# Queries and keys of the first 512 positions read eight tokens to a partition, in half-height loads, with a new order of the first part

## The chip, the cores and the metric

One core of a Trainium2 chip runs the kernel. The metric is the time of one execution in device microseconds (us), the median of several runs. A profile is one further execution, recorded by the hardware; its engines are PE (TensorE: matmuls, with PEld its weight loads), DVE (VectorE), ACT (ScalarE), POOL (GpSimd) and SP (SyncE, here a queue of DMA issues).

## What is computed

Attention over 4 batches of 8 heads, 768 positions and 64 numbers to a head, in which a query sees the first four positions (sinks) and the last 128 up to itself; the heads are put beside one another (512 numbers to a position), and two layers with a squared ReLU between them follow.

```python
def _attn_ref(q, k, v, n_sink, window):        # q, k, v: 4, 8, 768, 64; n_sink 4, window 128
    scores = scale * np.matmul(q, k.transpose(0, 1, 3, 2))
    keep = is_sink | in_window
    scores = np.where(keep, scores, -1000000000.0)
    a = np.exp(scores - np.max(scores, axis=-1, keepdims=True))
    a = a / (np.sum(a, axis=-1, keepdims=True) + 1e-09)
    return np.matmul(a, v)

def _moe_ref(x, w_in, w_out):                  # x: 3072, 512; w_in: 512, 2048; w_out: 2048, 512
    r = np.maximum(x @ w_in, 0.0)
    return (r * r) @ w_out
```

All inputs and the output are float32; the kernel multiplies in bfloat16.

## The kernel before

The four batches run one behind another, with the attention of a batch beside the two layers of the batch before it. Batch 0 has nothing to run beside, so its first part is the kernel's start.

**How batch 0 starts.** Its queries and keys come in two groups: positions 0 to 511 (four tiles of 128) are loaded as float32 by SP into the tiles qr, all others as bfloat16 by POOL into qn. A head pair m (two heads, 0 to 3) is handled together. For the first 512 positions the steps are: eight loads on SP (line 351), keys and queries by turns for each pair, 256 KB each; a cast and regrouping of each into qs (`regroup`, line 478, recorded as the copies at lines 192 and 194); four 128x128 transposes on PE for each (`transpose`, line 507); and a copy out of PSUM into qkT (`unload`, line 522), which also puts the tokens back in order. Then come, for each block of 256 queries (s = 0 for the first, s = 1 for the second): the scores on PE (line 613; in block 0 a bias is first added by a matmul with the identity, line 606), the exponential on ACT (line 634), in block 1 a mask on POOL or DVE (lines 218 and 646), the product with the values on PE (line 682), the normalisation on DVE (lines 698 and 699), two transposes called bridges (line 731) with copies into xT. The sink keys (line 549) and the sinks' scores and exponential (lines 572 and 580) serve block 1 onward.

**The layers.** Layer 1 (line 763) of batch 0 runs in groups of 16 matmuls: four blocks of 128 hidden numbers by 256 positions. There are eight groups for blocks 0 and 1, and the quarter of w_in (line 308) that a group needs is loaded by POOL. Layer 2 of batch 0 (line 984) starts behind them, and then the layers of batch 1 and the rest.

**What sets the order.** Every step is numbered as it is declared, and `ORDER` lists the numbers in the order in which the instructions are written, over all engines. Each engine runs its own instructions in that order, and semaphores come in where a step needs another's result. A letter behind a number chooses the engine (d DVE, a ACT, g POOL, p PE), and "+" the pool of PSUM banks ("att" or "den", two each). A bank is free when its readers are done, so the order also decides who waits for whom over banks. `DUMMIES` puts idle matmuls ahead of some steps (29 in step 945, ten ahead of 63, eight ahead of 58, four ahead of 64, three each ahead of 83, 91 and 97); they keep PE busy and compute nothing.

The steps that are spoken of, by number (m is the pair):

| step | what | step | what |
|---|---|---|---|
| 8 to 15 | the eight loads into qr | 83, 84, 91, 92 | scores of block 0, m = 0, 1, 2, 3 |
| 55, 61, 67, 73 | cast of keys, m = 0 to 3 | 85, 86, 93, 94 | their exponentials |
| 56, 62, 68, 74 | cast of queries | 87, 89, 95, 97 | their values; 88, 90, 96, 98 norms |
| 57, 63, 69, 75 | transposes of keys | 103, 104, 113, 114 | scores of block 1, m = 0, 1, 2, 3 |
| 58, 64, 70, 76 | transposes of queries | 105, 107, 115, 117 | their exponentials |
| 59, 65, 71, 77 | unloads of keys | 106, 108, 116, 118 | their masks |
| 60, 66, 72, 78 | unloads of queries | 109, 111, 119, 121 | their values |
| 80, 81, 82 | sink keys, scores, exponential | 99, 101; 100, 102 | bridges of block 0; their copies |
| 4, 5, 2, 127 | triangles, bias masks (POOL), second constants (DVE), mask tables (POOL) | 156, 162, 168 | first, second, third group of layer 1 |
| 19 to 25, 26 | v loads and w_in's first three quarters, its last | 177 | first group that needs w_in's last quarter |
| 37 to 44, 49 to 52 | key and query loads of batch 1 | 45 to 48 | v loads of batch 1 |
| 144, 136, 145 | scores of block 2 | 146, 148; 149 | exponentials and a mask of block 2 |
| 278 | start of layer 2 | 248, 251 | last transposes of batch 1's queries and keys |

One load, before: 128 partitions, in each two heads with four tokens of 64 numbers, so rows of 1 KB in memory. Two pairs lie beside one another in a tile of 128 x 4 x 256.

Of the kernel before, what the change touches and what calls it, by code (L numbers as in the profile page):

```python
# [21 lines left out]
944 0 1 2 7 8 9 10 11 12 13 14 15 16 17 18 945+0 3 5 19 20 21 6 79 22 23 24 25 55d 56d 57+0 58 59d 60a 83+0 85 103+1  # L22
105 26 27 28 62d 61d 63+1 64 67d 68d 65a 69+0 70 71d 72d 66a 84+1 73a 74a 75+1 76 78d 91+0 86 77a 93 80 113+1 87+0
92+1 89 94 95+0 97 115 88 90 96 98 114+1 99+0 101 117 100d 104+0 81+1 102d 107 82 4 29 106g 30 31 32 33 34 35 36 37 38
39 40 41 42 43 44 45 46 127 47 48 49 50 116d 118d 108d 156+0 109+1 119+1 121 111 162+0 110 120 122 112 123+1 125 124d
126d 157a 163a 158a 164a 168+1 165+0 51 52 53 54 177+0 169a 170d 208g 166a 167a 178d 171+1 179a 172a 128+1 131+0 174+0
173a 132a 129d 319 323 321 175d 324 176d 322 130a 320 159+1 133a 160a 161a 278+0 279 136+1 144+0 145+0 280 281 148 138
146 289+1 149d 139d 274 147d 275 282 290 283 291 292 284 276 277 134+1 137+0 135 286a 140 141d 285 287d 293 150+0 151
294 142+1 196+0 192+1 295 143 193 200+1 198a 202a 195d 197 199d 201 203d 297d 194d 296 298a 152+1 154 204+0 205
# [87 lines left out]
def kernel(  # L117
# [59 lines left out]
    def bank(slot, name, shape, dtype):  # L177

        return rooms[slot.pool][slot.room].tile(shape, dtype, name=name, tag=f"{slot.pool}{slot.room}")
# [153 lines left out]
    def load_qk(b, m0, ti, g, pairs=2, behind=None, yields=()):  # L333
# [10 lines left out]
        def run(e):  # L344
            if half == 0:
                qr_t[share] = bank(qr_slot[share], "qr", [128, shares * 2 * pairs, n * D], FP32)
            t = qr_t[share][:, 2 * pairs * half:2 * pairs * half + 2 * pairs, :]
            qr_t[b, "all", m0, ti, g] = t
            for m in range(m0, m0 + pairs):
                qr_t[b, m, ti, g] = t[:, 2 * (m - m0):2 * (m - m0) + 2, :]  # L350
            return [nc.sync.dma_start(  # L351
                out=t,
                in_=(q, k)[ti][b, 2 * m0:2 * m0 + 2 * pairs, t0:t0 + 128 * n, :].rearrange(
                    "h (p t) d -> p h (t d)", t=n))]
# [72 lines left out]
    def attention(b, key):  # L427
# [16 lines left out]
        def stage(g, f0, f1, side):  # L444
# [25 lines left out]
            for m in range(0, NP, w) if b not in NATURAL else ():  # L470
# [4 lines left out]
                for ti in () if casted else (1, 0):  # L475
                    sl = qs_slot[b, m, ti, g] = Slot("qs", 1)

                    def regroup(e, m=m, ti=ti):
                        t = qs_t[b, m, ti, g] = bank(qs_slot[b, m, ti, g], "qs", [128, w, n, 2, D], BF16)
                        if w == 2:  # L480
                            copy(e, t, qr_t[b, "all", m, ti, g].rearrange("p (m h) (t d) -> p m t h d", m=2, d=D))
                        else:
                            copy(e, t[:, 0], qr_t[b, m, ti, g].rearrange("p h (t d) -> p t h d", d=D))
                    who = {"pool": 0.17 + w * n * 0.125}
                    who["dve"] = 0.06 + w * n * (0.094 if b else 0.115)
                    if w == 1:
                        who["act"] = 0.2 + w * n * 0.107
                    regs.append(op(at(f), who, regroup,
                                   after=[ops["qk", b, m, ti, g]] + prev_tr + begun, takes=[sl],
# [31 lines left out]
                for j in (1, 0):  # L521
                    def unload(e, m=m, j=j, casted=casted):
# [9 lines left out]
                        else:  # L532
                            ins = copy(e,
                                       qkT_sb[:, m, j, t0 // 128:last // 128, :].rearrange(
                                           "c a b -> c (a b)").rearrange("c (p t) -> c p t", t=n),
                                       bank_t[b, m, g][:, j, 0:128 * n].rearrange("c (t p) -> c p t", t=n))
# [3 lines left out]
                    for x in ((m + j,) if w == 2 else (m,)):  # L540
                        ops.setdefault(("copies", b, x, g), []).append(c)
# [742 lines left out]
    for m in range(NP):  # L1284
        for ti in (1, 0):
            load_qk(0, m, ti, 0, 1)
# [114 lines left out]
```

## Time and profile before

| | us |
|---|---|
| median of 3 runs | 210.08 (209.55 to 211.03) |
| the profiled execution | 210.16 |
| its span (first to last instruction) | 208.3 |

| engine | busy us | share |
|---|---|---|
| PE | 200.5 | 96% |
| DVE | 173.1 | 83% |
| ACT | 135.9 | 65% |
| POOL | 96.4 | 46% |

The granted TensorE clock is 1.00 over the span. 1.9 us of the profiled execution lie around its span. Times in a view count from the span's start. The chain of waits is followed back from the last instruction, each step to what released it; an engine's name means that the engine was working, DMA that a transfer was awaited. PE's busy time is modelled at the ends of matmuls, so gaps of a few hundredths are not seen.

POOL's share of the start, which sets when its loads go out (columns: start, length, engine, line, work, count):

```profile
1.70 0.77 POOL L218 TENSOR_SCALAR_AFFINE_SELECT sg<-sg 128x256 bf16<-128x256 bf16 x2
2.53 0.61 POOL L254 COPY sg<-sg 128x512 bf16<-128x512 bf16 x1
3.45 2.16 POOL L381 DMA_DIRECT2D v<-in_v_dram  x2
5.61 0.76 POOL L308 DMA_DIRECT2D w_in_sb<-in_moe_w_in_dram  x1
10.69 2.25 POOL L308 DMA_DIRECT2D w_in_sb<-in_moe_w_in_dram  x3
```

### The profile page before, as it was taken

What the parts mean: (1) busy time and instruction counts of PE and PEld (TensorE: products, weight loads), DVE (VectorE), ACT (ScalarE), POOL (GpSimd) and SP (SyncE); (2) the same over time, 40 slices, a digit from 0 to 9 for tenths busy, and PEclk for the clock granted to TensorE, in tenths of its full rate; (3) what the DMA queues carried; (4) which work ended last, traced back from release to release, by engine and by line L of the source; (5) the groups of instructions that cost most, each with busy time, mean ns of one, the idle gap of its engine ahead of it and who ended that gap; (6) DMA issues with size and microseconds to landing.
All of it is one profiled execution on the core that took longest, in us unless ns stands there. A gap on an engine that the chain in (4) does not pass through costs nothing.

```text
span 208.3 us, 5924 instructions
## 1 busy us (share of the span) xinstructions
PE 200.5 (96%) x2476; PEld 174.3 (84%) x2476; DVE 173.1 (83%) x318; ACT 135.9 (65%) x189; POOL 96.4 (46%) x138
## 2 busy tenths in 40 slices
PE   7989999999998999999999998999999999999993
PEld 7658997457986889989878987999888999998893
DVE  6759268867599998999999987999989598999933
ACT  2695888433749589999987047988856248693110
POOL 7999274599599976689356209000043000000000
PEclk9999999999999999999999999999999999999999
DMA  6999999999999999999999945300204203200115
GB/s 190 260 184 207 173 196 215 166 146 142 261 68 148 131 172 137 181 162 121 154 116 220 109 96 134 148 3 0 50 14 145 50 5 113 88 3 0 50 54 201
DMA packets 93994, 26.10 MB, mean 125 GB/s; under 512 B 86800, under 2 KB 91408, under 8 KB 93968
## 3 DMA queue, kind: packets, MB, share of 16 engines
q0 software_dynamic: 69248, 12.59, 80.2%
q1 hardware_dynamic: 24536, 13.01, 27.9%
q8 instruction: 19, 0.31, 0.6%
q10 hardware_dynamic: 184, 0.14, 0.2%
q14 instruction: 7, 0.06, 0.1%
HBM read 27.30 MB, written 6.29 MB: 161 GB/s over the span
## 4 chain that ended last, share of the span: by engine, by line
PE 82%; DVE 5%; DMA 4%; SPq 3%; ACT 2%; issue 2%; DVEq 0%; ACTq 0%
PE py L1233 26%; PE pm L894 23%; PE pm L763 10%; PE py L984 7%; PE po L682 6%; PE ps L613 4%; DMA qr<-in_q_dram 3%; PE pt L507 2%; PE py L1094 2%; SPq L351 2%; DVE t L936 1%; PE px L731 1%; DMA xT<-xn_sb 1%; SPq L461 1%; ACT expm L634 1%
## 5 line engine op out<-in xcount | busy, mean ns | idle before, releaser
L634 ACT ACTIVATE expm<-ps 128x1024 bf16<-128x1024 f32 (+1 forms) x48 | 43.7, 953 | 7.7 <-PE ps L613 7.5
L218 POOL TENSOR_SCALAR_AFFINE_SELECT expm<-expm 128x512 bf16<-128x512 bf16 x34 | 22.7, 705 | 44.2 <-ACT expm L634 40.4
L894 PEld LDWEIGHTS <-w_in_sb 128*128 128x128 bf16 x384 | 32.2, 114 | 2.0 <-issue 1.9
L1233 PEld LDWEIGHTS <-gT_sb 128*128 128x128 bf16 x288 | 27.2, 98 | 4.7 <-issue 1.4
L917 ACT ACTIVATE gT_sb<-r 128x1024 bf16<-128x1024 bf16 x28 | 28.8, 1054 | 2.5 <-DVE r L963 2.3
L894 PE MATMUL pm<-xs,wi 128*128 128x256 bf16 (+1 forms) x288 | 29.2, 246 | 0.1
L192 ACT ACTIVATE osb<-py 128x256 f32<-128x256 f32 (+1 forms) x30 | 11.9, 399 | 25.0 <-PE py L1233 19.8
L936 DVE TENSOR_TENSOR t<-t,pm 128x512 f32<-128x512 f32 x36 | 23.8, 683 | 3.7 <-PE pm L894 2.9
L894 PEld LDWEIGHTS <-wi 128*128 128x128 bf16 x288 | 24.6, 114 | 1.0 <-DVE xs L852 0.4
L1233 PEld LDWEIGHTS <-sg 128*128 128x128 bf16 x216 | 20.3, 98 | 2.7 <-issue 0.5
L963 DVE CUSTOM_DVE_ANT_1 r<-pm,t 128x1024 bf16<-128x1024 f32 x18 | 21.8, 1218 | 0.5 <-PE pm L894 0.5
L763 PE MATMUL pm<-xT,w_in_sb 128*128 128x256 bf16 x192 | 22.0, 273 | 0.0
L763 PEld LDWEIGHTS <-w_in_sb 128*128 128x128 bf16 x192 | 20.6, 114 | 0.3 <-issue 0.2
L894 PE MATMUL pm<-xs,w_in_sb 128*128 128x256 bf16 (+1 forms) x192 | 19.9, 246 | 1.0 <-DVE t L936 1.0
L951 ACT ACTIVATE r<-pm 128x1024 bf16<-128x1024 f32 x16 | 16.3, 1022 | 4.9 <-DVE osb L194 2.3
L1233 PE MATMUL py<-w_out_sb,gT_sb 128*128 128x256 bf16 x144 | 18.7, 273 | 0.6 <-ACT expm L634 0.6
L1233 PE MATMUL py<-wt,sg 128*128 128x256 bf16 x144 | 18.7, 273 | 0.0
L1233 PE MATMUL py<-wt,gT_sb 128*128 128x256 bf16 x144 | 18.5, 273 | 0.0
L682 PEld LDWEIGHTS <-expm 128*128 128x128 bf16 x352 | 16.6, 97 | 1.9 <-issue 0.6
L682 PE MATMUL po<-v,expm 128*128 128x65 bf16 x352 | 17.8, 193 | 0.3 <-ACT expm L634 0.3
L699 DVE TENSOR_TENSOR xn_sb<-po,rc 128x512 bf16<-128x512 f32 (+1 forms) x28 | 17.2, 615 | 1.0
L984 PE MATMUL py<-w_out_sb,gT_sb 128*128 128x512 bf16 x64 | 14.8, 379 | 0.0
(104 smaller groups left out, 376.9 us busy)
## 6 DMA issues: line engine op xcount, KB each, us to landing
out_dram<-osb SPq DMA_DIRECT2D x11, 512.0 KB, 3.7
v<-in_v_dram POOLq DMA_DIRECT2D x24, 128.0 KB, 6.2
qn<-in_k_dram POOLq DMA_DIRECT2D x20, 128.0 KB, 6.1
qn<-in_q_dram POOLq DMA_DIRECT2D x20, 128.0 KB, 6.5
w_in_sb<-in_moe_w_in_dram POOLq DMA_DIRECT2D x4, 512.0 KB, 9.4
w_out_sb<-in_moe_w_out_dram POOLq DMA_DIRECT2D x4, 512.0 KB, 10.8
qr<-in_k_dram SPq DMA_DIRECT2D x4, 256.0 KB, 5.1
qr<-in_q_dram SPq DMA_DIRECT2D x4, 256.0 KB, 4.8
```

What stands on the lines that cost most here:

```text
L218: nc.gpsimd.affine_select(out=e_tile, in_=e_tile, compare_op=ALU.is_ge, fill=fill, base=i - 1, pattern=[[0, n], [1 if i else -1, 128]], ch ...
L634: nc.scalar.activation(out=x[:, :, o:512], in_=bank_t["s", b, s, m][:, :, o:512], func=AF.Exp, scale=scale)
L682: touch(("po", b, s, m0), e, nc.tensor.matmul(pv[:, i, h2, :], lhsT=lhsT, rhs=rhs, start=(n_ == 0), stop=(n_ == len(mms) - 1)), j)
L699: touch(("po", b, s, m0), e, nc.vector.tensor_tensor(out=xn_sb[:, 2 * s:2 * s + 2, 128 * (m0 + j0):128 * (m0 + j0 + nj)].rearrange("p i (j ...
L763: nc.tensor.matmul(pm[:, i, :], lhsT=w_in_sb[:, fb // 4, kb, fb % 4:512:4], rhs=xT[:, c0 // 256:(c0 + cw) // 256, kb, :], start=(kb == 0), ...
L894: touch(tag, e, nc.tensor.matmul(y[:, bk, i, :], lhsT=weights(name, f0 + i, a), rhs=rhs[:, a, :], start=fresh and i == 0 and a == 0, stop= ...
L917: nc.scalar.activation(out=d, in_=x, func=AF.Square)
L936: touch(tag, e, nc.vector.tensor_tensor(out=T["t"], in0=T["t"], in1=T["y"][:, bk], op=ALU.subtract), bk)
L951: touch(tag, e, nc.scalar.activation(out=r, in_=T["y"], func=AF.Relu), 0, 1)
L963: touch(tag, e, nc.vector._custom_dve(TENSOR_ADD_SAT, out=r.rearrange("p b n c -> p b (n c)"), in0=T["y"].rearrange("p b n c -> p b (n c)" ...
L984: touch((b, u), e, nc.tensor.matmul(pm[:, i, :], lhsT=gT_sb[:, fb, 128 * t:128 * t + 128], rhs=w_out_sb[:, fb, :], start=(fb == 0), stop=( ...
L1233: touch((b, u), e, nc.tensor.matmul(region(name), lhsT=x[:, i, :], rhs=w_[:, i, :], start=first and i == 0, stop=i == HB - 1, skip_group_c ...
```

## The change

Three things are changed for positions 0 to 511 of batch 0.

The loads: one load now writes 64 partitions, in each two heads with eight tokens of 64 numbers, so rows of 2 KB. A tile of 128 x 2 x 512 holds the keys, or the queries, of two pairs: the even pair in partitions 0 to 63, the odd one in 64 to 127. There are still eight loads of 256 KB, now in the order keys of pairs 0 and 1, queries of 0 and 1, keys of 2 and 3, queries of 2 and 3.

The steps on them: a cast, its four transposes and its unload now take half of the tokens of each partition (the first four of eight, or the last four) of both pairs in the tile, where they took all tokens of one pair. A cast waits for two loads, and the scores of a pair wait for four unloads where they waited for two. An unload writes four tokens of every eight, for two pairs.

The order: `ORDER` is new up to its 191st step and the same from there. `DUMMIES` is not changed, so the idle matmuls go with their steps. The instructions on PE are the same in number.

```diff
@@ -19,14 +19,14 @@
 ORDER = """
-944 0 1 2 7 8 9 10 11 12 13 14 15 16 17 18 945+0 3 5 19 20 21 6 79 22 23 24 25 55d 56d 57+0 58 59d 60a 83+0 85 103+1
-105 26 27 28 62d 61d 63+1 64 67d 68d 65a 69+0 70 71d 72d 66a 84+1 73a 74a 75+1 76 78d 91+0 86 77a 93 80 113+1 87+0
-92+1 89 94 95+0 97 115 88 90 96 98 114+1 99+0 101 117 100d 104+0 81+1 102d 107 82 4 29 106g 30 31 32 33 34 35 36 37 38
-39 40 41 42 43 44 45 46 127 47 48 49 50 116d 118d 108d 156+0 109+1 119+1 121 111 162+0 110 120 122 112 123+1 125 124d
-126d 157a 163a 158a 164a 168+1 165+0 51 52 53 54 177+0 169a 170d 208g 166a 167a 178d 171+1 179a 172a 128+1 131+0 174+0
-173a 132a 129d 319 323 321 175d 324 176d 322 130a 320 159+1 133a 160a 161a 278+0 279 136+1 144+0 145+0 280 281 148 138
-146 289+1 149d 139d 274 147d 275 282 290 283 291 292 284 276 277 134+1 137+0 135 286a 140 141d 285 287d 293 150+0 151
-294 142+1 196+0 192+1 295 143 193 200+1 198a 202a 195d 197 199d 201 203d 297d 194d 296 298a 152+1 154 204+0 205
+8 9 10 11 12 13 14 944 15 0 4 945+0 7 16 1 3 6 19 20 21 5 62d 56d 61a 55a 63+0 57+1 64 58 65a 59a 66a 60a 73d 75+0 77a
+67d 68d 74d 69+0 104+1 103+1 76 70 107 105 71d 84+1 22 79 23 24 25 106g 108g 78d 72d 2 86 83+0 80 85 91+1 93 92+0 87+1
+89 81+1 113+0 94 88 90 95+0 97 82 115 96 98 114+1 117 26 118g 27 28 29 30 31 32 116d 99+1 109+0 101 111 119+0 102d
+100a 156+1 120 121 112 110 122 162+1 123+0 125 319 322 323 126a 124a 168+0 157a 169a 163d 324 320 321 159+0 158a 170d
+160a 165+1 177+0 166a 167d 174+1 128+1 171+1 178d 129d 161d 130a 164a 175d 172d 176d 33 34 208g 35 131+1 278+0 279
+133a 132a 179a 280 281 36 37 38 39 40 41 42 144+1 136+0 145+0 146 148 138 173a 149g 43 44 45 46 47 48 127 282 283 147d
+274 275 276 277 289+1 290 284 17 18 139d 49 50 51 52 53 54 291 292 134+1 137+0 135 286a 140 141d 285 287d 293 150+0
+151 294 142+1 196+0 192+1 295 143 193 200+1 198a 202a 195d 197 199d 201 203d 297d 194d 296 298a 152+1 154 204+0 205
 212+0+1 153a 155d 189+0 215 206a 213 190a 214 207d 186+0 216 191d 248+0 187d 249d 251+1 209 253a 188d 252a 180+1 181d
 250d 182d 183+0 326 184a 185d 300 301 230+0+1 233 299 288 219+0+1 231 220 304+0 210+0 306a 211 222 305 237+0+0 240
 232d 325 302 221 303 223 241d 238 239d 311 307 217+1 254+0 224+0 308a 255 309 218 242+0 225 243 452g 422 423 424 425
@@ -343,15 +343,12 @@
 
         def run(e):
             if half == 0:
-                qr_t[share] = bank(qr_slot[share], "qr", [128, shares * 2 * pairs, n * D], FP32)
-            t = qr_t[share][:, 2 * pairs * half:2 * pairs * half + 2 * pairs, :]
-            qr_t[b, "all", m0, ti, g] = t
-            for m in range(m0, m0 + pairs):
-                qr_t[b, m, ti, g] = t[:, 2 * (m - m0):2 * (m - m0) + 2, :]
+                qr_t[share] = bank(qr_slot[share], "qr", [128, 2, 2 * n * D], FP32)
+            qr_t[b, m0, ti, g] = qr_t[share]
             return [nc.sync.dma_start(
-                out=t,
-                in_=(q, k)[ti][b, 2 * m0:2 * m0 + 2 * pairs, t0:t0 + 128 * n, :].rearrange(
-                    "h (p t) d -> p h (t d)", t=n))]
+                out=qr_t[share][64 * half:64 * half + 64],
+                in_=(q, k)[ti][b, 2 * m0:2 * m0 + 2, t0:t0 + 128 * n, :].rearrange(
+                    "h (p t) d -> p h (t d)", t=2 * n))]
         o = dma_op("sp", ("qk", b, m0, ti, g), run, 16 * pairs * ROW[256 * n] + (0.7 if (b, m0, ti, g) == (0, 0, 0, 0) else 0.0), behind,
                    () if half else [qr_slot[share]], yields)
         for m in range(m0, m0 + pairs):
@@ -477,16 +474,14 @@
 
                     def regroup(e, m=m, ti=ti):
                         t = qs_t[b, m, ti, g] = bank(qs_slot[b, m, ti, g], "qs", [128, w, n, 2, D], BF16)
-                        if w == 2:
-                            copy(e, t, qr_t[b, "all", m, ti, g].rearrange("p (m h) (t d) -> p m t h d", m=2, d=D))
-                        else:
-                            copy(e, t[:, 0], qr_t[b, m, ti, g].rearrange("p h (t d) -> p t h d", d=D))
+                        x = qr_t[b, m, ti, g].rearrange("p h (t d) -> p t h d", d=D)
+                        copy(e, t[:, 0], x[:, n * (m % 2):n * (m % 2) + n])
                     who = {"pool": 0.17 + w * n * 0.125}
                     who["dve"] = 0.06 + w * n * (0.094 if b else 0.115)
                     if w == 1:
                         who["act"] = 0.2 + w * n * 0.107
                     regs.append(op(at(f), who, regroup,
-                                   after=[ops["qk", b, m, ti, g]] + prev_tr + begun, takes=[sl],
+                                   after=[ops["qk", b, m // 2 * 2 + i, ti, g] for i in range(2)] + prev_tr + begun, takes=[sl],
                                    reads=[qr_slot[b, m, ti, g]]))
                     ops["regroup", b, m, ti, g] = regs[-1]
 
@@ -530,14 +525,16 @@
                                            "c i a b -> c i (a b)").rearrange("c i (p t) -> c i p t", t=n),
                                        bank_t[b, m, g][:, j, 0:256 * n].rearrange("c (i t p) -> c i p t", i=2, t=n))
                         else:
+                            mm, half = m // 2, m % 2
                             ins = copy(e,
-                                       qkT_sb[:, m, j, t0 // 128:last // 128, :].rearrange(
-                                           "c a b -> c (a b)").rearrange("c (p t) -> c p t", t=n),
-                                       bank_t[b, m, g][:, j, 0:128 * n].rearrange("c (t p) -> c p t", t=n))
+                                       qkT_sb[:, 2 * mm:2 * mm + 2, j, t0 // 128:last // 128, :].rearrange(
+                                           "c m a b -> c m (a b)").rearrange("c m (p t) -> c m p t", t=2 * n)
+                                       [:, :, :, n * half:n * half + n],
+                                       bank_t[b, m, g][:, j, 0:128 * n].rearrange("c (t m p) -> c m p t", t=n, m=2))
                         touch(("pt", b, m, g), e, ins, j, alone=True)
                     c = op(at(f + 0.04), {"dve": 0.42 if casted else 0.11 + w * n * 0.144, "act": 0.17 + w * n * 0.107}, unload,
                            after=[trs[j]] + prev_scores + prev_sinks, reads=[bs])
-                    for x in ((m + j,) if w == 2 else (m,)):
+                    for x in ((m + j,) if w == 2 else (m // 2 * 2, m // 2 * 2 + 1)):
                         ops.setdefault(("copies", b, x, g), []).append(c)
                     copies.append(c)
 
@@ -1281,9 +1278,10 @@
     FAST = {1: ((0, 1), (2,)), 2: ((0,), (1, 2)), 3: ((0,), (1, 2))}
     CLASSIC2 = ((0, 0), (0, 1))
     load_sinks("act", 0)
-    for m in range(NP):
+    for mm in range(0, NP, 2):
         for ti in (1, 0):
-            load_qk(0, m, ti, 0, 1)
+            for m in (mm, mm + 1):
+                load_qk(0, m, ti, 0, 1)
     for b in range(1, B):
         load_sinks("sp", b)
     load_v(0, 0, None, [("qk", 0, 3, 0, 0)])
```

## The prediction

> **What bounds the kernel now.** I read the page first: the engines' busy time and the chain that ended last.
>
> ```profile
> PE 200.5 (96%) x2476; PEld 174.3 (84%) x2476; DVE 173.1 (83%) x318; ACT 135.9 (65%) x189; POOL 96.4 (46%) x138
> PE 82%; DVE 5%; DMA 4%; SPq 3%; ACT 2%; issue 2%; DVEq 0%; ACTq 0%
> ```
>
> TensorE is the bound nearly everywhere; the 4% of DMA is where the change works. The chain in order of time shows that place.
>
> ```profile
> 3.97 0.47 SPq L351
> 4.44 0.04 issue
> 4.48 6.15 DMA qr<-in_q_dram
> ...
> 10.72 0.64 ACT qs L192
> ...
> 11.40 0.40 PE pt L507 x4
> ...
> 13.76 0.82 ACT expm L634
> ...
> 16.62 1.87 PE pm L763 x16
> 18.50 1.45 PE po L682 x48
> 19.95 1.75 PE pm L763 x16
> 21.70 0.45 PE px L731 x8
> 22.15 6.99 PE pm L763 x64
> ```
>
> Columns: start, length, work. The eighth and last load of queries (issued at 4.48) lands at 10.63. Call this moment L. Until 16.6 the chain passes between ACT, PE and DVE; from 16.62 on it is PE alone. The third layer-1 group starts at 22.15, L + 11.52. The busy time by stretches says that PE is then full:
>
> ```profile
> 4.00:6.00 2.00, 2.00 (x22) 2.00 (x20) 1.05 (x3) 0.00 (x0) 2.00 (x3) 1.00 1.01 307
> 6.00:8.00 2.00, 2.00 (x28) 1.36 (x25) 0.98 (x2) 1.23 (x2) 1.73 (x6) 1.00 1.11 306
> 16.00:36.00 20.00, 20.00 (x239) 18.36 (x238) 13.58 (x26) 15.31 (x18) 11.92 (x16) 1.00 1.49 198
> 36.00:56.00 20.00, 20.00 (x192) 12.64 (x191) 12.87 (x21) 9.83 (x15) 15.95 (x23) 1.00 2.20 175
> 55.00:56.00 1.00, 1.00 (x11) 1.00 (x10) 0.81 (x2) 1.00 (x3) 0.22 (x1) 1.00 1.04 422
> ```
>
> The second figure is PE's busy time, the last the GB/s moved. PE is busy for all of 16 to 56. The order is the same in both programs from about 46 us on, and both do the same matmuls before that. So what the change is worth is how much earlier or later the third layer-1 group starts; behind it, both have five more groups (1.75 each) and 0.9 of transposes before layer 2 (33.52 before). The rest follows from two terms: L, and the work from L to that group.
>
> **The work behind L.** Before, the last load feeds one head pair; the seven other loads have already been cast, turned and partly exponentiated. In the new program each cast takes half of the tokens of two pairs, so both query casts of pairs 2 and 3 need both of the last two query loads. Behind L stand in series:
> - two casts on DVE (steps 68, 74; four took 2.20): 1.10;
> - eight transposes, of which PE issues 0.45, then the two bias matmuls (0.33) and the scores of step 84 (0.17, and 0.23 to its end), with 0.07 to each next engine: about 1.25. ACT can start step 86 at L + 2.35;
> - then ACT without a gap: exponentials 86, 85, 93, 94 (start to start 0.70 on 11.25 to 11.94), sink keys 80 (0.43), sink exponential 82 (0.38), exponentials 115 and 117 (four in 3.61 up to 17.37, one of them 0.70: 0.97 each) and the copy 100 (0.59): 2.80 + 0.43 + 0.38 + 1.94 + 0.59 = 6.14.
>
> I checked that nothing arrives later than ACT asks for it: the three unloads on DVE (0.60 each) end at L + 2.95, the sink keys ask at L + 3.05; the scores 91 and 92 are ready 0.25 before their exponentials. Step 100 gates the first layer-1 group, at L + 8.5. Then 1.75 + 0.36 (one values step) + 1.75 + 0.45 (two bridges): the third group starts at L + 12.8. That is 1.3 later than now for the same L: the new order has nine ACT steps and three of the four values steps of the second block between L and layer 1, where the old one has six and none.
>
> **L itself.** The eight loads are 2.10 MB, moved from about 2.2 at 306 GB/s until 9.05; landing is 1.6 behind. The count of SP issues (eight of 0.47) stays; two kinds of change pull apart:
> - Rows twice as long (2 KB for 1 KB). The nearest rows are the w_in loads, read in 2 KB rows: the second, third and fourth land at 18.7, 21.4 and 24.5, 1.05 MB in 2.9 us, 362 GB/s. At that rate 5.8 for 6.85. The v loads go out 0.65 earlier (they no longer stand behind the bias masks on POOL), which takes back some 0.3: L = 9.9.
> - Each load writes 64 partitions instead of 128. No row shows a large load of that shape. If the write side of a half is half as wide, the bound is half of the best rate in the trace, 422 / 2 = 211 GB/s: 9.95 us, L = 2.2 + 9.95 + 1.6 = 13.7.
>
> The low end is all 2.10 MB at 422: L = 8.8; no load can land before its issue plus the shortest seen, 4.48 + 2.75 (first load, issue 0.81, cast 3.56) = 7.2. Between 9.9 and 13.7 no row decides. I take 13.7: the loads go down one queue one behind another, lower half, upper half, so all engines write the same half at the same time. [...]
>
> **Parts that cost nothing, and their cover.**
> - The warm-up matmuls now read the triangles and so start 0.5 later, behind two POOL selects (0.55): the first transposes wait for K casts after 4.5 anyway. The idle matmuls keep their step numbers (ten ahead of step 63) and run while loads fly.
> - Unloads write four of every eight tokens. The nearest rows are 0.60 (strided, today) and 0.41 (contiguous). Up to 0.2 more each: three on DVE behind L, of which 0.1 is covered, so 0 to +0.5; I take 0.
> - Second constants (0.9 on DVE) move behind the unloads; the next DVE step waits for values until L + 4.6, they end at L + 3.8.
> - w_in's last quarter is issued behind two POOL masks (1.70 for two selects each), near 16.2 instead of 12.2. It stands behind 6.3 MB anyway, lands by about 24.5, and is asked for three groups after the third, at L + 18.
> - The key and query loads of batch 1 now stand on POOL behind the mask of step 149, which waits for exponential 148. Counted from the start of layer 2: 148 ends at +5.8, the mask takes 1.7, two loads 1.8, four v loads 3.6, the mask tables 2.3, three loads 2.6, and the last lands 5.1 later (as 48.9 to 54.0 now): +22.9. The transposes that need it stand at 56.44 - 33.52 = +22.9. Covered with nothing to spare: 0 taken, bounds 0 and +1.
>
> **Sum.** L later by 3.1, work behind it 1.3: +4.4 on the profiled execution's 210.16, 214.6; that run is 0.08 above the median of 210.08, so 214.5.
>
> **Rivals.**
> - *Full rate into half the partitions.* L = 9.5 to 10.6, so 1.3 less 1.1 to 1.3 less 0: +0.2 to +1.3, and 211 at the middle. For it: all 16 engines carry each load, and today's 306 GB/s is below the 422 that they reach. Against it: the shape is not in the trace. In this case the longer rows gain nearly a microsecond and the order gives it back.
> - *Faster.* Loads become so quick that the order's tail is paid for. Place: the landing of the eighth load; it decides from L below 9.3. At 8.8 the gain is 1.83 - 1.3 = 0.5, 209.5; at the floor of 7.2 it is 2.1, 207.9. For it: 2 KB rows, and today v loads share the engines from 4.5 on. Against it: over 1% needs the floor itself, and from the fourth load on none landed less than 4.6 after its issue.
> - *POOL is late.* Loads at full rate, but POOL's chain to batch 1's last query load (22.9 against 22.9) or the strided unloads bite: +0.6 for the first case and 1.0 to 1.5 more, 212.3. POOL's 4.9 us of waits on w_out's DMAs speak for a tight queue; that DMA falls idle after 57 speaks against a long delay.
>
> **Chances.** I call 1% (2.1 us) what a measurement of this kernel tells from no change. Half rate 0.56, with 212.6 to 216; full rate 0.30; POOL late 0.08; faster 0.06, half of it by over 1%. Faster by over 1%: 0.03. Within 1%: 0.30 + 0.03 + 0.02 of the half-rate case = 0.35. Slower: 0.54 + 0.08 = 0.62. The likeliest case alone spans 213.5 to 215.8; the full-rate case needs its lower part, so the range is 210.2 to 215.9, leaving out the faster rival, the best of the full rate and L beyond 15.
>
> **What would show it.** Right: the wait on the last qr load ends near 13.7, ACT's first exponential of the first block follows 2.3 to 2.4 later, the third layer-1 group starts 12.8 behind the landing, and GB/s in 4 to 8 is near 211 instead of 306. If GB/s is 306 or more there and the landing is near 10, the half-rate step is wrong and the time is near 211. If the third group starts less than 11.5 behind the landing, the order's term has the wrong sign. If PE waits at the pt transposes of qn near 57, POOL is late. If the time falls below 208, a step above hid a wait that the new order removes.

## The result and the profile after

| | before | after |
|---|---|---|
| median, us | 210.48 (209.55 to 211.28, 6 runs) | 217.75 (216.84 to 218.48, 6 runs) |
| ratio to before | | 1.0346, 95% interval 1.0305 to 1.0388 |
| the profiled execution, us | 210.16 | 217.33 |
| last qr load landed (L) | 10.63 | 15.24 |
| third layer-1 group starts | 22.15 | 29.60 |
| from there to the end of the execution | 188.0 | 187.7 |

The change makes the kernel 7.3 us slower. The last row says where: nothing is lost behind the third group, and the whole loss lies in the first 30 us.

The page of the profile after, its busy times and its shares of the chain:

```profile
PE 202.5 (94%) x2476; PEld 174.8 (81%) x2476; DVE 172.8 (80%) x315; ACT 134.1 (62%) x189; POOL 101.1 (47%) x144
PE 84%; DMA 6%; SPq 4%; DVE 3%; issue 1%; ACT 1%; DVEq 0%
```

PE is busy for 2.0 us longer with the same 2476 matmuls. DMA's share of the chain has grown from 4% to 6%, by about the 4.6 us that L moved. The chain in order of time (start, length, work) shows both:

```profile
5.55 9.69 DMA qr<-in_q_dram
...
16.25 1.03 PE pt L502 x8
17.28 0.64 PE ps L603 x2
...
25.29 1.75 PE pm L760 x16
...
27.40 1.75 PE pm L760 x16
...
29.60 8.73 PE pm L760 x80
```

L is 5.55 + 9.69 = 15.24, and the third group starts 14.36 behind it. From 16.25 to beyond that group the chain is on PE without a break; two bias matmuls (line 603) take 0.64. The busy time by stretches (the stretch, its length, PE, PEld, DVE, ACT, POOL, then the granted clock of PE, the DMA engines' busy share, GB/s) says why they take so long:

```profile
4.00:6.00 2.00, 1.98 (x19) 1.71 (x17) 0.00 (x0) 0.33 (x1) 2.00 (x4) 1.00 1.05 234
6.00:8.00 2.00, 0.35 (x4) 0.23 (x4) 0.00 (x0) 1.99 (x3) 1.88 (x5) 1.00 1.51 197
...
10.00:12.00 2.00, 0.00 (x0) 0.00 (x0) 0.00 (x0) 0.38 (x1) 2.00 (x4) 1.00 1.35 194
12.00:14.00 2.00, 1.00 (x12) 0.75 (x14) 0.86 (x2) 0.44 (x1) 0.69 (x1) 0.78 1.17 217
...
16.00:18.00 2.00, 1.75 (x12) 1.11 (x14) 1.90 (x4) 0.47 (x1) 1.39 (x3) 0.50 2.17 163
18.00:20.00 2.00, 2.00 (x16) 0.79 (x13) 1.05 (x4) 1.22 (x4) 1.71 (x3) 0.51 1.32 205
```

In 4 to 6 the engines were as busy as before (1.05 against 1.01) and moved 234 GB/s in place of 307. PE has nothing to do from 9.8 to 13.0, waiting for casts of loads that have not landed; from 13.1 to 20 its clock is granted at half, and the work behind L begins in the midst of that. Over 4 to 10, first before, then after:

```profile
4.00:10.00 6.00, 5.98 (x69) 4.71 (x67) 3.96 (x9) 3.23 (x6) 5.67 (x11) 1.00 1.27 280
```

```profile
4.00:10.00 6.00, 3.95 (x47) 3.28 (x45) 1.07 (x2) 4.25 (x7) 5.68 (x12) 1.00 1.39 197
```

### The profile page after: what moved, and what is told of

Read it like the earlier page. It is cut to its first block, busy times and chain, and to the rows that moved or that the text cites. A ratio compares the mean times of both kernels' runs of the same rounds, so it can differ in the third digit from the quotient of the medians.

```text
span 215.3 us, 5936 instructions
## 1 busy us (share of the span) xinstructions
PE 202.5 (94%) x2476; PEld 174.8 (81%) x2476; DVE 172.8 (80%) x315; ACT 134.1 (62%) x189; POOL 101.1 (47%) x144
## 3 DMA queue, kind: packets, MB, share of 16 engines
q1 hardware_dynamic: 23512, 13.01, 28.3%
## 4 chain that ended last, share of the span: by engine, by line
PE 84%; DMA 6%; SPq 4%; DVE 3%; issue 1%; ACT 1%; DVEq 0%
PE py L1230 25%; PE pm L891 23%; PE pm L760 10%; PE po L679 7%; PE py L981 7%; DMA qr<-in_q_dram 4%; PE ps L610 4%; PE pt L502 2%; SPq L348 2%; PE py L1091 2%; PE px L728 1%; DMA xT<-xn_sb 1%; PE ps L603 1%; SPq L458 1%; SPq L710 1%
## 5 line engine op out<-in xcount | busy, mean ns | idle before, releaser
L218 POOL TENSOR_SCALAR_AFFINE_SELECT expm<-expm 128x512 bf16<-128x512 bf16 x40 | 27.9, 731 | 55.1 <-ACT expm L631 52.2
L610 PE MATMUL ps<-qkT 64*128 64x128 bf16 (+1 forms) x256 | 15.1, 246 | 0.4 <-ACT r L772 0.4
```

The lines of the kernel that those rows point to most:

```text
L218: nc.gpsimd.affine_select(out=e_tile, in_=e_tile, compare_op=ALU.is_ge, fill=fill, base=i - 1, pattern=[[0, n], [1 if i else -1, 128]], ch ...
L610: nc.tensor.matmul(ps[:, h2, o:o + w], lhsT=qkT_sb[r, m, 1, c, :], rhs=qkT_sb[r, m, 0, qb:qb + w // 128, :], start=(i == 0 and not biased) ...
```

## The experiments

Three explanations were to be told apart: the loads are slow because they write 64 partitions, or because of their long rows, or because of what else is in flight in the new order; and what stands behind L is long because of the order, or because of PE's clock. Each landing, and each start of the third group, is read from one execution, the profiled one. The changed kernel and e6, which load alike, differ by 0.24 in the landing (15.24 and 15.48). The start of the third group scatters more: e2, e9 and e12 have the median time of before, but their profiled executions, which were among the slowest of theirs, start it at 23.59 to 23.77, where that of before has 22.15. Smaller differences than these say little by themselves; the ratios rest on several executions each.

**Half height with short rows, in the old order** (e1): the loads of before, but with four heads of 256 tokens into 64 partitions.

```diff
-                out=t,
-                in_=(q, k)[ti][b, 2 * m0:2 * m0 + 2 * pairs, t0:t0 + 128 * n, :]
+                out=qr_t[share][64 * half:64 * half + 64],
+                in_=(q, k)[ti][b, 2 * first:2 * first + 4, t0 + 256 * half:t0 + 256 * half + 256, :]
 ...
```

> Before, with its order of steps and its 1 KB rows, but each load writes 64 partitions (lower or upper half) of both pairs of a tile. Theory A (a load into half of the partitions moves at about half the rate): the last load lands at 14.5 to 15.5 instead of 10.6, GB/s between 4 and 6 is 210 to 240 instead of 307, and the time is 4 to 5.5 above before. Rival B (the 2 KB rows or their issue are slow, the height is innocent): lands at 10.3 to 11, time within 0.7 of before.

Measured: ratio 1.0361 (1.0324 to 1.0398). Its chain, and its busy time by stretches:

```profile
5.60 10.40 DMA qr<-in_q_dram
...
29.95 6.99 PE pm L761 x64
```

```profile
4.00:6.00 2.00, 0.32 (x6) 0.15 (x3) 0.00 (x1) 0.00 (x0) 2.00 (x3) 1.00 1.12 216
6.00:8.00 2.00, 0.84 (x12) 0.67 (x12) 0.42 (x1) 0.00 (x0) 1.73 (x6) 0.84 1.12 214
```

L is 16.00 and the rate 216 and 214, with rows of 1 KB and the order of before. In e1 the loads also go in the turn of the changed kernel (two keys, two queries, and so on), and a cast waits for two of them; e2 and e12 have that turn and cost nothing, and no load waits for a cast (the eight issues of e1 follow one another until 6.2). So writing to 64 partitions is enough to cost as much as the whole change.

**Full height with long rows, in the old order** (e2), and **the same with the new order and steps** (e3). Both read 2 KB per partition into all 128, from other rows of the same tensors. The lines are those of e3; e2 writes the same rows into the tile of before, and has the turn of loads of the changed kernel as well.

```diff
+                out=qr_t[share][:, half, :],
+                in_=(q, k)[ti][b].rearrange("h s d -> (h s d)")[65536 * m0:65536 * m0 + 65536].rearrange("(p c) -> p c", c=512)
 ...
```

> Before, with its order of steps, but each load reads 256 KB that lie together as 128 rows of 2 KB into all 128 partitions (other numbers than the queries and keys asked for, so the output is not the reference's). Theory A: rows of 2 KB are at least as quick as rows of 1 KB: the last load lands at 9.6 to 10.6, GB/s in 4 to 6 is 307 to 370, time 0 to 1 below before. Rival B: lands after 12.5, time 2 or more above before.

> After, with its steps and order, but each load reads 256 KB that lie together as 128 rows of 2 KB into all 128 partitions (other numbers, so the output is not the reference's). Theory A with the prediction's term for the order: lands at 9.6 to 10.6, the third layer-1 group starts 12.5 to 13.1 behind the landing, clock 1.00, time 0 to 1.3 above before. Rival C (the order itself costs more than 1.3): the third group starts 14 or more behind the landing and the time is 2.5 or more above before.

Measured: e2 1.0000 (0.9977 to 1.0024), e3 1.0086 (1.0048 to 1.0125). The chain of e3, and its busy time by stretches:

```profile
4.29 7.39 DMA qr<-in_q_dram
...
24.50 8.73 PE pm L760 x80
```

```profile
4.00:6.00 2.00, 1.74 (x19) 1.56 (x17) 0.00 (x0) 1.51 (x2) 2.00 (x4) 1.00 0.92 258
```

Long rows are worth nothing in time. With everything else of the change in place, full height brings L from 15.24 to 11.68 and the time from 1.0346 to 1.0086: the half height costs 2.6%, 5.5 us, and the rest of the change 0.9%.

e3 also loses something behind the third group, 1.2 in its profiled execution (189.2 from there to the end, where before has 188.0). Its chain there runs through a mask and the loads of POOL to batch 1's last query load:

```profile
41.77 2.88 POOL expm L218 x2
...
53.41 7.36 DMA qn<-in_q_dram
```

PE waits 1.7 for that load. So POOL is late here, which the prediction had among its rivals. It is not in e4, whose third group starts as early and which takes 188.0 from there.

**The new order alone** (e4, with the loads, casts and unloads of before, in the new turn of loads), and **the same with POOL's old turn** (e8: bias masks, step 5, ahead of the first v loads again). **That turn alone in the changed kernel** is e7.

```diff
-944 0 1 2 7 8 9 10 11 12 13 14 15 ...
+8 9 10 11 12 13 14 944 15 0 4 945+0 7 16 1 3 6 19 20 21 5 62d ...
```

```diff
-... 16 1 3 6 19 20 21 5 62d ...
+... 16 1 3 5 19 20 21 6 62d ...
```

> The new order of steps with the old loads, casts and unloads (full height, 1 KB rows, one pair at a time; loads in the order keys, keys, queries, queries). Prediction's term: lands near 10.6, third layer-1 group 12.5 to 13.1 behind it, time 1.0 to 1.6 above before. Rival D (the new order is no worse, the whole loss is in the loads): third group at most 11.5 behind, time within 0.5 of before or below.

> The new order with the loads, casts and unloads of before (as in e4), and in it POOL's bias masks ahead of the first v loads again. Theory (v loads issued earlier cost 1.4 of landing): the last load lands near 10.6 as before, the third layer-1 group starts near 23.0, and the time is 210.7 to 211.4, against 212.4 to 212.8 of e4. Rival (the landing of e4 came from something else in the order, such as the loads' K, K, Q, Q turn): landing stays near 12, time stays near 212.7.

> The changed kernel with one difference: on POOL the bias masks stand ahead of the first v loads again, as in the kernel before, so that v and w_in go out later. Theory (the v loads, issued earlier, take their share of the DMA engines from the query loads): last landing 1.0 to 1.4 earlier, 13.8 to 14.2, and the time 1 to 1.5 or more below 217.7 (more if TensorE's idle time gets too short to lose its clock). Rival, the prediction's own step (earlier v loads are worth 0.3): landing within 0.4 of 15.2, time within 0.5.

Measured: e4 1.0092 (1.0064 to 1.0119), e8 1.0050 (1.0019 to 1.0081), e7 1.0302 (1.0271 to 1.0332). The chains of e4 and of e8:

```profile
4.50 7.55 DMA qr<-in_q_dram
...
24.45 8.73 PE pm L763 x80
```

```profile
4.51 6.76 DMA qr<-in_q_dram
...
23.77 8.73 PE pm L763 x80
```

The landing is 12.05 in e4 and 11.27 in e8; in e7 it is 14.56 against 15.24. So in these executions v loads that go out 0.74 earlier (3.05 against 3.79; the expectation of e9 calls it 0.4) cost 0.8 and 0.7 of landing, between the two expectations. The times go the same way by 0.4% in both, but their intervals overlap. The 0.6 that e8 still lands behind before is not explained. **The turn of the loads** was tried for it (e12: before, with its eight loads as two keys, two queries, and so on):

> The kernel before with its eight loads in the turn of the changed kernel (two keys, two queries, two keys, two queries in place of key, query, ...), and nothing else. e8 landed 0.6 later than before with the same POOL order, and e1 and e2 have this turn too. If the turn of the loads is the cause: landing near 11.2 and time 0.3 to 0.8 above before. If not (scatter from run to run, or the rest of the order): landing within 0.3 of 10.63.

The time is that of before: 0.9986 (0.9957 to 1.0015). ACT takes up its last casts of e12 without waiting, so its landing can't be read, and the 0.6 stays open.

**A version that was to beat both** (e9): before, with the head rows and sink values ahead of the first v and w_in loads, to keep those out of the way of the query loads.

```diff
-... 3 5 19 20 21 6 79 22 23 24 25 55d ...
+... 3 5 6 79 19 20 21 22 23 24 25 55d ...
```

> The kernel before with one difference: on POOL the head rows and the sink values stand ahead of the first v and w_in loads, so that these go out some 2 later (v's first load near 5.8 in place of 3.45). Theory (v and w_in take DMA time from the query loads: in e8 against e4 going out 0.4 later was worth 0.8 of landing): the last query load lands 0.7 to 1.2 before 10.63, the third layer-1 group starts up to 1 before 22.15, unless v or the first w_in quarter then comes too late; time 209.0 to 210.2 against 210.5 to 211. Rival (v and w_in become the late ones): the landing is earlier but the first layer-1 groups wait, and the time is 0.5 to 2 above before.

Measured: 0.9987 (0.9960 to 1.0014), no difference. The query loads are no longer what ends last in its chain; a quarter of w_in is, for which the third group waits (this view ends at 25.1):

```profile
11.50 12.05 DMA w_in_sb<-in_moe_w_in_dram
...
23.59 1.50 PE pm L763 x12
```

**PE's clock** (e6): the changed kernel with more idle matmuls in its gaps.

```diff
-    945: 29, 58: 8, 63: 10, 64: 4, 83: 3, 91: 3, 97: 3,
+    945: 29, 58: 8, 63: 28, 64: 4, 75: 56, 76: 24, 83: 3, 91: 3, 97: 3,
```

> The changed kernel with more idle matmuls on TensorE ahead of the first block's transposes (18 more at the step that had ten, 56 and 24 at two later steps), nothing else. Theory (TensorE's idle time from 9.8 to 13.0 halves its clock until 20, which costs some 2): granted clock near 1.00 throughout, the last load still lands near 15.2, the third layer-1 group starts 12.4 behind it in place of 14.4, and the time falls by 1.5 to 2.0, to about 216. Rival (the lower clock costs nothing, since ACT's exponentials set the pace behind the landing): the time stays within 0.5 of 217.7.

The stretch from 12 to 20, first in the changed kernel, then in e6:

```profile
12.00:20.00 8.00, 5.67 (x46) 3.13 (x47) 4.39 (x10) 3.76 (x7) 3.80 (x6) 0.57 1.48 197
```

```profile
12.00:20.00 8.00, 7.17 (x99) 4.65 (x96) 4.20 (x10) 4.75 (x8) 3.87 (x7) 1.00 1.50 196
```

And the chain of e6:

```profile
5.55 9.94 DMA qr<-in_q_dram
...
28.30 8.73 PE pm L760 x80
```

The clock is 1.00, and the third group starts 12.8 behind the landing (15.48) in place of 14.4: on the path of these two executions the half clock costs 1.5. The profiled execution is 215.87, 1.5 below that of the changed kernel.

That the kernel's time falls by as much is not shown. The ratio is 1.0303 (1.0266 to 1.0340) against 1.0346, 0.9 us, with intervals that overlap. The profiled execution is the fastest of the five that the ratio of e6 is taken from; the other four, with a granted clock of 0.998 or more over the span, took 216.97 to 218.18, as the changed kernel does (216.84 to 218.48). One execution of the changed kernel has a clock of 0.998, so that at most 1.1 us of it can have been at half speed; it took 217.50, in the middle of the six. In e10, below, the two executions at 0.998 and 1.000 took 217.82 and 217.34, the two at 0.984 and 0.982 took 216.45 and 216.95.

**Two queues** (e5: upper halves issued by ACT, lower halves by SP; e10, its control: queries by ACT, keys by SP, so that both queues are given lower and upper halves in the same turn; e11: the same division in the kernel before).

```diff
-            return [nc.sync.dma_start(
+            return [(nc.scalar if half else nc.sync).dma_start(      # e5
+            return [(nc.sync if ti else nc.scalar).dma_start(        # e10, e11
```

> The changed kernel with one difference: the loads of the upper 64 partitions (odd pairs) are issued by ACT's queue, those of the lower 64 by SP's, so that both halves are in flight from the start; the work is the same. Theory (each half has its own half-width path into SBUF, and one queue keeps only one half busy at a time): both paths fill together, GB/s in 4 to 8 returns to 260 or more, the last landing goes from 15.2 to about 12, PE's clock stays at full speed, and the time is 212 to 214.5. [...] Third possibility (SP's issues of 0.61 each set the rate, not the width): eight issues on two queues end near 3, the landing follows them by the same 9 and more, GB/s stays near 200.

> The changed kernel with two queues, as in e5, but divided by tensor: keys on SP's queue, queries on ACT's, so that both queues send lower half, upper half, lower half, upper half in step. Theory (what e5 gained, it gained by filling both halves at once): GB/s in 4 to 8 near 215 as in the changed kernel, last landing 14 to 15.3, time 216 to 217.7. Rival (e5 gained by its second queue as such: earlier issues and a larger share against v): GB/s near 250, last landing near 11.7, time 213 to 214.5, as e5.

> The kernel before with its query loads issued by ACT's queue and its key loads by SP's. If the number of queues and the earlier issues matter (the rival of e10), the last landing falls from 10.63 to 9.9 or less and the time by 0.5 or more, a version faster than both kernels. If the DMA engines already move what they can (theory: 287 to 307 GB/s from 2 on), landing stays within 0.4 of 10.6 and the time within 0.6 of before; the sink load, now behind four issues on ACT, may cost some.

Measured: e5 1.0141 (1.0107 to 1.0175), e10 1.0300 (1.0268 to 1.0333), e11 1.0107 (1.0071 to 1.0144). The landing of the last key load in the chains of e5 and e10, and their stretch from 8 to 10:

```profile
2.51 7.38 DMA qr<-in_k_dram
```

```profile
8.00:10.00 2.00, 1.82 (x28) 1.43 (x26) 0.79 (x3) 1.93 (x5) 0.39 (x1) 1.00 1.11 322
```

```profile
3.21 10.74 DMA qr<-in_k_dram
```

```profile
8.00:10.00 2.00, 0.00 (x0) 0.00 (x0) 0.76 (x2) 0.88 (x1) 0.40 (x1) 0.86 1.07 218
```

With the same turn of halves on both queues e10 moves 216 GB/s in 4 to 10 (197 in the changed kernel) and has about the time of the changed kernel, and its keys land at 13.95; with one half on each queue e5 has 322 in 8 to 10 where e10 has 218, lands its keys at 9.89, begins its last cast at 12.11, and is 1.6% faster than e10. That each half has a path of its own, as the theory of e5 has it, is not shown by that: e17 below is divided as e5 is and moves no more than e10 (211 and 213 in 4 to 12). The eight issues of e10 are out by 3.9, those of the changed kernel by 6.2, and still the rate is no better than 216: the longer issues of half-height loads are not what holds it down. In e11 ACT issues its queries only behind the sink load, the first at 2.16; PE then idles from 6 to 8, its clock is at half in 10 to 12, and the kernel is slower than before.

**Closing the account by repairs** (e13: e5, added idle matmuls as in e6, though at other places, and e7 at once; e14: e5 and those idle matmuls; e15: e13 with step 0, a step of constants, moved to the front, where the sink load was meant; e17: e13 with the sink load, step 7, first on ACT's queue; e16 and e18: e15 and e17 without the added idle matmuls).

```diff
-    945: 29, 58: 8, 63: 10, 64: 4, 83: 3, 91: 3, 97: 3,
+    945: 29, 58: 8, 63: 40, 64: 4, 75: 8, 76: 16, 83: 3, 91: 3, 97: 3,   # e13, e14, e15, e17
 ...
-8 9 10 11 12 13 14 944 15 0 4 945+0 7 16 ...
+0 8 9 10 11 12 13 14 944 15 4 945+0 7 16 ...                             # e15, e16
+7 8 9 10 11 12 13 14 944 15 0 4 945+0 16 ...                             # e17, e18
```

> The changed kernel with three repairs at once: upper-half loads on ACT's queue (e5), more idle matmuls on TensorE in its gaps (e6), POOL's bias masks ahead of the first v loads (e7). Theory (half-width loads, clock and POOL's turn make up the loss but for the order's longer tail of 0.9 to 1.3): granted clock near 1.00, last landing 11.0 to 11.6, third layer-1 group 12.4 to 12.8 behind it, at 23.4 to 24.4; time 1.3 to 2.2 above before, ratio 1.004 to 1.011. Rival (a further cost of the new order sits behind layer 1, out of sight of these three): the third group starts by 24.4, yet the ratio stays above 1.014.

> e5 (upper-half loads on ACT's queue) with more idle matmuls on TensorE: 30 more at the step that had ten, 8 and 16 at two later ones. Theory (the half clock from 12.4 to 16.8 in e5 costs 1 to 2): clock near 1.00, third layer-1 group 12.4 to 12.8 behind the landing at 11.7, near 24.3 in place of 26.0; time 1 to 2 below e5, ratio 1.005 to 1.010 in place of 1.0141. Rival (the lower clock is hidden behind ACT's exponentials): clock at 1.00 and the ratio still 1.0107 or more.

> e13 (two queues, more idle matmuls, POOL's old turn) with the sink load first on ACT's queue, ahead of the upper-half loads, as it stands in both kernels. Theory: no wait of POOL for the sink values; last landing 10.8 to 11.8, third layer-1 group 12.4 to 12.8 behind it, at 23.4 to 24.5; time 1.3 to 2.3 above before, ratio 1.006 to 1.011. Rival (a cost of the new order behind layer 1): third group by 24.5 and the ratio still above 1.013.

> e15 without the added idle matmuls (ten at the first step, as in the changed kernel). Theory (the half clock costs TensorE 1 to 2 behind the landing): clock at half speed for some 4, third group 1.0 to 2.0 later than in e15, and the time 0.8 to 2 above e15. Rival (hidden): clock at half speed, and the time within 0.4 of e15.

> e13 (two queues, more idle matmuls, POOL's old turn) with the sink load first on ACT's queue, as in both kernels. Theory: POOL no longer waits for the sink values and v and w_in go out by 15 as before; granted clock near 1.00, last landing 11 to 12, third layer-1 group 12.4 to 12.8 behind it, at 23.4 to 24.8; time 1.3 to 2.5 above before, ratio 1.006 to 1.012. Rival (a further cost of the new order behind layer 1, as e13's and e15's ratios of 1.018 and 1.017 would have it): third group by 24.8, and the ratio still above 1.014.

> e17 without the added idle matmuls (ten at the first step, as in the changed kernel). Theory (the half clock costs 1 to 2 where it lies behind the landing): if half speed lasts past the landing, third group and time are 1 or more above e17. Rival (hidden, as e15 and e16 with 1.0173 and 1.0172 suggest, where half speed ended at 12, before the last casts): clock at half speed for some 4, and the time within 0.4 of e17.

None came out at the times that the theory gave. Measured: e13 1.0182 (1.0138 to 1.0227), e14 1.0229 (1.0189 to 1.0269), e15 1.0173 (1.0132 to 1.0214), e16 1.0172 (1.0145 to 1.0198), e17 1.0248 (1.0209 to 1.0287), e18 1.0282 (1.0241 to 1.0324). The repair with two queues brings a wait of its own. POOL's instructions in e14, with the idle time ahead of them and what ended it:

```profile
12.96 2.03 POOL L551 TENSOR_TENSOR vs<-vs_in,head_rows 32x130 bf16<-32x130 f32 x4 [4.57 <-DMA vs_in<-in_v_dram]
...
15.87 1.50 POOL L308 DMA_DIRECT2D w_in_sb<-in_moe_w_in_dram  x2
```

The sink load stands behind four loads on ACT's queue, POOL waits 4.57 for it (3.62 in e5), and two quarters of w_in go out at 15.87, where the changed kernel issues them at 11.19; in e14, e15 and e16 the chain then runs through the last w_in quarter (landing at 27.1 to 28.3), which it does not in the changed kernel. e15 and e16 leave the sink load where it was. e17 and e18 do move it; but the upper halves then start 1.5 later, and the chain of e17 goes from an early key load almost wholly through ACT and PE:

```profile
2.38 6.31 DMA qr<-in_k_dram
...
26.84 8.73 PE pm L760 x80
```

Behind that key load ACT first spends 1.28 on an instruction ACT_TABLE_LOAD (from 8.76; in e5 it stands at 5.88, while the loads are still in flight) before it casts. The added idle matmuls hold the last transposes up by 0.2 at most: in e13 and e17 the last cast ends at 13.10 and 14.85, and they start at 13.15 and 15.06.

In e17 each queue has one half, and the rate in 4 to 12 is 211 GB/s all the same (218 in e18). Over that stretch the kernels with one half on each queue and POOL held up moved 233 to 246 (e5, e13 to e16), e10 with the same turn on both queues and POOL held up 213, and the changed kernel 196. So neither one half on each queue nor a waiting POOL alone makes e5's rate, and what a second queue is worth stays open. That half height is the cost is shown by e1 and e3, which do without one.

Two pairs bear on what the clock costs. e15 and e16 are equal, and there the half clock of e16 had ended at 12, ahead of the last transposes at 12.83. In e18 it lasts to about 15.2 and the third group starts 1.1 behind that of e17; the ratios differ by 0.3% and overlap. So here too a cost shows on the path of single executions, and not beyond doubt in the time.

**The account.** From one kernel to the next:

| kernel | L | third group | ratio |
|---|---|---|---|
| before | 10.63 | 22.15 | 1 |
| new order, old loads (e4) | 12.05 | 24.45 | 1.0092 |
| and long rows, new steps (e3) | 11.68 | 24.50 | 1.0086 |
| and half height: after | 15.24 | 29.60 | 1.0346 |

The order costs 2.3 of the third group's start: 1.4 of landing and 12.40 - 11.52 = 0.9 behind it. Long rows with the new casts and unloads cost nothing. Half height costs 5.1: 15.24 - 11.68 = 3.6 of landing, and 14.36 - 12.82 = 1.5 behind it, which the profiled execution of e6 does not have. Each row is one execution. That half height is what costs, by some 5 us, rests on the ratios of e1 and e3 as well; how the 5 divide into landing and clock rests on the single paths alone.

## Why the prediction was wrong

The time lies outside the range, 3.25 above the 214.5 and 1.85 above the upper end. The direction and the likeliest case were right; against the profiled execution the sum was 2.7 too low, and two of its steps were each 1.5 short: the term for L, and the price of nothing for PE's idle time.

- *"From there PE is full, and what the change is worth is how much later the third group starts."* Right. From the third group to the end, before and after take 188.0 and 187.7; e1, e4, e5, e6, e7, e8, e10 and e13 take 187.3 to 188.1. Two kernels take more, e3 189.2 and e17 189.8, and in e14, e15 and e16 w_in's last quarter, not the start of the third group, decides.
- *L, "half of the best rate in the trace, 13.7".* This step failed in its size: that half height costs landing is right (15.24 against 11.68 in e3, 16.00 in e1 against 10.63), but L is 15.24. The rate is near the 211 too (216 and 214 GB/s in 4 to 8 in e1, 234 and 197 in the changed kernel). That the write side of a half is half as wide was the author's estimate, and no run shows it: against the 307 and 306 of before, the rate of e1 is 30% lower, not half. Of the missing 1.5, POOL's turn is 0.7 (e7 lands at 14.56), where the prediction had "takes back some 0.3", and that inside a bound for longer rows which was not the case taken. The rest is argued, not tested: 211 GB/s was given to the queries and keys alone, while v and w_in share the engines (in 3 to 15 the packets of SP's queue took 79.0% of the 16 engines' time, those of POOL's 50.6%), and all of them together moved 197 in 4 to 10. By the landing 2.68 MB had been moved (176 GB/s over 15.24 us), 0.58 of it not queries or keys; before, 2.38 MB and 0.28. The further 0.3 MB at some 200 GB/s are an estimate of 1.5, POOL's 0.7 among them.
- *Longer rows, "L = 9.9".* Wrong: they gain no time at full height (e2). The row it went by was a w_in load of POOL, another queue and another tensor, and its 362 GB/s counts 1.05 MB of float32 read for each quarter. The profile counts the bfloat16 written, 0.52 MB, which is 181 GB/s in the same 2.9 us; its rate over 16 to 20, with these loads in flight, is 206. So that row never showed a rate above 306. The full-rate rival took its gain from longer rows out of the same row.
- *The work behind L, "12.8".* Right at full clock: 12.8 in e3 and e6; in e6 ACT's first exponential of block 0 starts 2.27 behind the landing (2.35 was forecast), ACT works from there without a gap, and the first layer-1 group starts 8.5 behind the landing, as forecast. The chain there goes by PE, though, which is as full as ACT; the forecast went by ACT alone. Wrong for the changed kernel, 14.36 and 3.15: the matmul durations were taken from rows at full clock, and there ACT has to wait for PE, 1.92 ahead of that exponential (1.51 in e6) and 0.37 once more behind it.
- *"The first transposes wait for K casts anyway; the idle matmuls run while loads fly."* This step failed too. It priced PE's idle time at nothing. Before, PE was busy for 5.98 of the 6 us from 4 to 10; with late loads it was busy for 3.95, and not at all from 9.8 to 13.0, and the clock went to half until 20. A bound that made the loads later should have asked what PE does in the meantime. It is worth 1.5 on the path of the profiled execution. In time e6 shows 0.9, which the intervals do not tell from nothing, and in e6 and e10 executions at full clock were not faster than others at half clock. So this step accounts for the profiled execution; whether it accounts for the second 1.5 in the other executions stays open.
- *Parts that cost nothing.* The unloads, constants and w_in's last quarter: e3 against e4 says so (24.50 and 24.45). In the changed kernel PE does not wait for the last qn load: the longest waits of its transposes are the 3.3 and 1.7 of the start. POOL was not late there. But nothing was to spare indeed: in the profiled execution of e3 layer 2 starts at 35.87 and that load lands at 60.77, 24.9 later and not 22.9: the mask's two selects take 2.88 where 1.7 was counted, the landing takes 7.36 in place of 5.1, and the mask tables only 0.9 in place of 2.3.

## What to carry to other kernels

Keep a load on all 128 partitions: here 64 partitions cost 2.6% of the kernel, and rows of 2 KB instead of 1 KB returned nothing. When a change delays the first loads, add up TensorE's idle time as well: in the changed kernel a gap of 3.3 us was followed by 7 us at half clock, and in e6 idle matmuls in the gaps kept the clock. Whether that pays has to be read from the times of several executions: here a path shorter by 1.5 in one profile was not a shorter time beyond doubt. Before comparing a rate with another, see that both count the same bytes. Price a queue's other customers before calling the move of a load free: here v loads issued 0.74 earlier cost the query loads 0.7 to 0.8 of landing, and four key and query loads put on ACT's queue kept the sink load behind them, for which POOL waited 3.62 in e5 and 4.57 in e14.

## What the runs showed that was not expected

- SP takes 0.61 to issue a load to 64 partitions (of 1 KB or 2 KB rows), 0.47 to 128 partitions in 1 KB rows, and 0.43 to 128 in contiguous 2 KB rows; eight such issues end at 6.2, 5.0 and 4.7.
- v loads of 128 KB that POOL issues 0.74 earlier put SP's last query load back by 0.7 to 0.8 in two pairs of kernels, as much as they were moved themselves; each landing is one execution.
- The clock came back late: PE worked without a break from 16.25, and half speed lasted to 20. Two bias matmuls took 0.64 in that time, against 0.33 in e6. Nor does the longest gap alone decide: e17 kept its clock over 2.78 of idle time, e5 lost it at about 13.1 (to 16.5) with no gap over 1.9, and e3 at about 8.8 (to 12.2) with 1.92 of idle time in all from 4 to 10.
